# Raw float32 scores for the first 14 head pairs, and theta and channel weights split by column blocks

## The chip, the cores and the metric

The kernel runs on one core of one Trainium2 chip. The metric is device time of one execution in microseconds (us); below, the time of a kernel is the median of its runs. The engines are named as the profile names them: PE (TensorE, matmuls; PEld its weight loads), DVE (VectorE), ACT (ScalarE), POOL (GpSimd) and SP (SyncE, which issues all DMAs here).

## The reference

Attention with soft-capped scores over 8 batches of 12 heads (448 tokens, 64 channels a head), and then a block that mixes tokens and channels:

```python
scores = cap * np.tanh(scale * (q @ k.T) / cap)
attn = softmax(scores)                       # over the last axis
x = concat_heads(attn @ v)                   # (8, 448, 768)

theta = x @ w_theta                          # 768 x 768
zr, zi = x * cos(theta), x * sin(theta)
u = x + w_tok_r @ zr + w_tok_i @ zi          # over the 448 tokens
out = u + max(u @ w_ch, 0)                   # 768 x 768
```

All inputs and the output are float32. `q` and `k` are drawn 5.5 times, `w_theta` and `w_tok_i` 8 times as large as usual.

## The kernel before

**Formats.** A matmul in float32 proper (`F32`) is issued as two instructions; one in `fp32r` (`F32R`) is issued as one, with operands of fewer bits. Where the kernel wants float32 accuracy from fp32r it splits each operand into `hi` (rounded to fp32r) and `lo` (the rest) and adds three products, hi·hi + lo·hi + hi·lo. Scores, theta, token mixing and the channel projection are done so. `attn @ v` (tile `a`, L229) and the sums of the exponentials (tile `r`, L244, a product with a column of ones) are products in float32 proper.

**Weights.** The host passes each weight matrix as words that hold more than float32, and the kernel makes `hi` and `lo` from them on the chip. A `Split` has three steps: `load` (a DMA on SP), `scale` (one pass on ACT, L99) and `split` (six passes on DVE and the rounding to `hi`, which ACT does for the channel weights, L109, and DVE for the others, L111). There are 6 pieces of theta weights (`th0` to `th5`, each 128 rows of the matrix), 7 of token weights (`tk0` to `tk6`) and 6 of channel weights (`c00` to `c02` for the left half of the columns, `c10` to `c12` for the right, each 256 rows). Theta and channel pieces pass through `g_sb[0]` and `g_sb[1]`, which theta also uses for its angles, so that two such pieces at most are in flight; token pieces pass through the buffers of `zh` and `zl`.

**Pairs and steps.** Work on attention goes by pairs of heads, `k` = 0 to 47, six for each batch. The pipeline runs in steps `s`: step `s` computes the scores of pair `s` in two halves (`qk_half`, tile `s`, L190, then tanh from PSUM to SBUF, L191, on ACT), and `attn @ v` and the sums of pair `s - 1`. The two heads of a pair lie on partitions 0 to 63 and 64 to 127, so that each score matmul uses 64 rows of the array. A half has 2 chunks x 3 products x 2 heads = 12 matmuls. Scores have one PSUM tile (4 banks), so that a half can start when the tanh of the half before is done. The exponentials (`exp_half`, L197) follow on ACT, the reciprocal of the sums (L271) every second step on DVE.

The first 8 steps (`FIRST`) do attention alone. From step 8 on, steps come in groups of six, one group for a batch (`part` 0 to 5): theta in parts 0 and 1, transposes and token mixing in parts 1 to 3, the channel projection in parts 4 and 5, each beside the attention of pair `s`. So batch 0 has its theta in steps 8 and 9 and its channel projections in steps 12 and 13.

**q and k.** `load_qk(k)` brings a pair into the one buffer `qk_sb`; `prep(k)` makes `hi[k]` and `lo[k]` from it on DVE (L176, L177) and then issues the load of the next pair. In the start, `prep` runs two steps ahead, later one.

**Order.** The order is written by hand, and each engine and the DMA queue take their instructions in that order. In a step: `qk_half(s, 0)`; weights at "a" (in the start only); `exp_half(s, 0)` (in the start); `av(s - 1)`; the load of v; sums; `qk_half(s, 1)`; `prep`; weights at "b"; the reciprocal; the script of the part, with the exponentials in it; weights at "c" ahead of the script's last item. The table `WEIGHTS` says which steps of which pieces stand there: `>` is load, `*` is scale, a bare name is split.

Of the kernel before, what the change touches and what calls it, by code (L numbers as in the profile page):

```python
# [12 lines left out]
F32 = mybir.dt.float32  # L13
F32R = mybir.dt.float32r
I32 = mybir.dt.int32
U32 = mybir.dt.uint32
AF = mybir.ActivationFunctionType
ALU = mybir.AluOpType

P = 128  # L20
# [6 lines left out]
FIRST = 8  # L27

DIRECT = 10


@with_exitstack
def softcap_attn_then_spectral_mix(ctx, tc, qk2, v, cap, w_theta, w_tok, w_ch, ident, outT):
    nc = tc.nc
    B, NP, P, _, S = qk2.shape
    D = P // 2
    CP = v.shape[2]
    NCH = S // CP
    DM = NP * P
    NJ = DM // P  # L40
    NC2 = 2 * S // P
    NS = B * NP

    const = ctx.enter_context(tc.tile_pool(name="const", bufs=1))
    wk = ctx.enter_context(tc.tile_pool(name="wk", bufs=2))
    psS = ctx.enter_context(tc.tile_pool(name="psS", bufs=1, space=bass.MemoryType.PSUM))
    psM = ctx.enter_context(tc.tile_pool(name="psM", bufs=4, space=bass.MemoryType.PSUM))

    w_theta, w_tok = (w.bitcast(I32).rearrange("j p (n two) -> j p n two", two=2) for w in (w_theta, w_tok))
    w_ch = w_ch.bitcast(I32).rearrange("h j p (n two) -> h j p n two", two=2)  # L50


    cap_sb = const.tile([P, 1], F32, name="cap_sb")
# [11 lines left out]
    wth_h = const.tile([P, NJ, DM], F32R, name="wth_h")  # L65
    wth_l = const.tile([P, NJ, DM], F32R, name="wth_l")
    wch_h = const.tile([P, NJ, DM], F32R, name="wch_h")
    wch_l = const.tile([P, NJ, DM], F32R, name="wch_l")
# [6 lines left out]
    qk_sb = const.tile([P, 2, S], F32, name="qk_sb")  # L75
# [36 lines left out]
            nc.vector.tensor_tensor(t, t, hi.bitcast(F32), op=ALU.subtract)  # L112
            nc.vector.tensor_tensor(lo, t, lw, op=ALU.add)

    def room_g(a, n, i):
        def room():
            st = g_sb[i % 2].rearrange("p x y s -> p (x y s)")
            raw = st[:, : 2 * a * n].rearrange("p (a n two) -> p a n two", a=a, two=2)
            return raw, st[:, 2 * a * n : 3 * a * n].rearrange("p (a n) -> p a n", a=a)
        return room  # L120

    def room_z(n, name):
        def room():
            raw = wk.tile([P, NC2, P], F32, tag="zh", name=f"{name}_raw", bufs=2).rearrange("p c s -> p (c s)")
            t = wk.tile([P, NC2, P], F32, tag="zl", name=f"{name}_t", bufs=2).rearrange("p c s -> p (c s)")
            return raw[:, : 2 * n].rearrange("p (n two) -> p n two", two=2), t[:, :n]
        return room

    hw = DM // 2
    steps = {}  # L130

    def weight_steps():
        for j in range(NJ):
            steps["th", j] = Split(room_g(1, DM, j), w_theta[j].unsqueeze(1), wth_h[:, j : j + 1], wth_l[:, j : j + 1])
        for c in range(NC2):
            steps["tk", c] = Split(room_z(S, f"swk{c}"), w_tok[c], wtk_h[:, c], wtk_l[:, c])
        for half in range(2):
            for i in range(NJ // 2):
                js, cols = slice(2 * i, 2 * i + 2), slice(half * hw, half * hw + hw)
                steps[f"c{half}", i] = Split(room_g(2, hw, half + i), w_ch[half, js].rearrange("a p n two -> p a n two"),  # L140
                                             wch_h[:, js, cols], wch_l[:, js, cols], True)


    WEIGHTS = {
# [6 lines left out]
    }  # L151

    def weights(s, pos):
        for word in WEIGHTS.get((s, pos), "").split():
            step = steps[word[-3:-1], int(word[-1])]
            {">": step.load, "*": step.scale}.get(word[0], step.split)()


    hi, lo, vt, pt, pst, bc = {}, {}, {}, {}, {}, {}
    X = {}  # L160
    state = {}

    def load_qk(k):

        nc.sync.dma_start(qk_sb, qk2[k // NP, k % NP])

    def load_v(k):
        vt[k] = wk.tile([CP, 2, NCH, D], F32, tag="v", name=f"v{k}", bufs=2)
        nc.sync.dma_start(vt[k], v[k // NP, k % NP])

    def prep(k):

        for parts, name in ((hi, "hi"), (lo, "lo")):
            tag, bufs = ("xhl", 6) if k < NP or k == NP + 1 else (name, 1)
            parts[k] = wk.tile([P, 2, S], F32R, tag=tag, name=f"{name}{k}", bufs=bufs)
        nc.vector.tensor_copy(hi[k], qk_sb)  # L176
        nc.vector.tensor_tensor(lo[k], qk_sb, hi[k].bitcast(F32), op=ALU.subtract)  # L177
        if k + 1 < NS:
            load_qk(k + 1)

    def qk_half(k, half):

        sp = psS.tile([P, 2, 2, 512], F32, tag="s", name=f"s{k}_{half}")
        pp = pt[k, half] = wk.tile([CP, 2, 2, S], F32, tag="p", name=f"p{k}_{half}", bufs=3)
        for i in range(2):
            ks = slice((2 * half + i) * CP, (2 * half + i + 1) * CP)
            for n, (kk, qq) in enumerate(((hi, hi), (lo, hi), (hi, lo))):
                for hh in range(2):
                    rows = slice(hh * D, (hh + 1) * D)
                    nc.tensor.matmul(sp[:CP, i, hh, :S], kk[k][rows, 1, ks], qq[k][rows, 0, :], start=n == 0, stop=n == 2)  # L190
        nc.scalar.activation(pp, sp[:CP, :, :, :S], AF.Tanh, scale=qscale[:CP])  # L191

    def exp_half(k, half):
# [30 lines left out]
    def av(k):  # L224
        va = vt.pop(k)
        acc = psM.tile([P, 512], F32, tag="m", name=f"a{k}")
        for c in range(NCH):
            for hh in range(2):
                nc.tensor.matmul(acc[hh * D : (hh + 1) * D, :S], va[:, hh, c, :], pt[k, c // 2][:, c % 2, hh, :],  # L229
                                 start=c == 0, stop=c == NCH - 1)  # L230
        x = wk.tile([P, S], F32, tag="x", name=f"x{k}", bufs=12)
        nc.scalar.copy(x, acc[:, :S])
        X[k // NP, k % NP] = x
# [132 lines left out]
    def us(b, j):  # L366
        split_x(b, j, "us")

    def pipeline(general):
        state["general"] = general  # L370
        load_v(0)
        prep(0)
        for step in (("tk", 0), ("tk", 1)):
            steps[step].load()

        prep(1)
        for s in range(FIRST + 6 * B):
            k = s - 1
            b, part = divmod(s - FIRST, 6)
            live = s < NS  # L380
            start = s < FIRST
            if s + 2 < FIRST:
                prep(s + 2)
            elif s == FIRST - 1:
                prep(FIRST)
            if live:
                qk_half(s, 0)
            if start:
                weights(s, "a")
                exp_half(s, 0)  # L390
            if 0 <= k < NS:
                av(k)
            if not start and part == 4:
                for j in range(NJ // 2, NJ):
                    us(b, j)
            if s + 1 < NS:
                load_v(s + 1)
            if 0 <= k < NS:
                sums(k, (0,) if start else (0, 1))
                if not start:  # L400
                    invert(k)
            if live:
                qk_half(s, 1)
            if 0 <= k and start:
                sums(k, (1,))
            if not start and s + 1 < NS:
                prep(s + 1)
            weights(s, "b")
            if 0 <= k and start:
                invert(k)  # L410
            script = ["B", "a", "b"] if start else part_scripts(b)[part]
            for i, e in enumerate(script):
                if not start and i == len(script) - 1:
                    weights(s, "c")
                    if s % 2 == 1 and s <= NS + 1:
                        norm(s - 3)
                        norm(s - 2)
                if isinstance(e, str):
                    if live:
                        if e in "AB":  # L420
                            exp_half(s, "AB".index(e))
                        else:
                            add_half(s, "ab".index(e))
                else:
                    e[0](b, e[1])
            if start:
                weights(s, "c")
                for n in {4: (0, 1), 5: (2, 3), 7: (4, 5)}.get(s, ()):
                    norm(n)
                for j in {6: range(4), 7: range(4, NJ)}.get(s, ()):  # L430
                    split_x(0, j, "xs")
# [50 lines left out]
```

## Time and profile before

| | |
|---|---|
| median of 3 runs | 1002.59 us (1002.05 to 1004.07) |
| the profiled execution | 1001.84 us, its span 999.8 us |
| mean granted TensorE clock | 0.987 |
| busy: PE, DVE, ACT | 961.5, 654.1, 598.1 us |
| q and k loads (L165) | 48 of 448 KB, 3.4 us to landing |
| theta and channel weight loads (L95) | 12 of 768 KB, 4.2 and 4.6 us to landing |

The profile is that of one execution; its time is set beside its span, which goes from the first to the last instruction on the core. A row of the order of time reads: start, length, engine, line, operation, output <- inputs, partitions x columns and shape, count, and in brackets how long the engine had been idle and what ended it. Neighbouring instructions of one kind are merged into a row, the length then reaching from the first start to the last end. `L190` is line 190 of the kernel before.

### The profile page before, as it was taken

What the parts mean: (1) busy time and instruction counts of PE and PEld (TensorE: products, weight loads), DVE (VectorE), ACT (ScalarE), POOL (GpSimd) and SP (SyncE); (2) the same over time, 40 slices, a digit from 0 to 9 for tenths busy, and PEclk for the clock granted to TensorE, in tenths of its full rate; (3) what the DMA queues carried; (4) which work ended last, traced back from release to release, by engine and by line L of the source; (5) the groups of instructions that cost most, each with busy time, mean ns of one, the idle gap of its engine ahead of it and who ended that gap; (6) DMA issues with size and microseconds to landing.
All of it is one profiled execution on the core that took longest, in us unless ns stands there. A gap on an engine that the chain in (4) does not pass through costs nothing.

```text
span 999.8 us, 12973 instructions
## 1 busy us (share of the span) xinstructions
PE 961.5 (96%) x5304; PEld 709.9 (71%) x5304; DVE 654.1 (65%) x893; ACT 598.1 (60%) x615; POOL 0.4 (0%) x6
## 2 busy tenths in 40 slices
PE   6988998969999999999999999999999999999897
PEld 2433676747677777877877877776778677789897
DVE  4999777777676568656585576675586566753551
ACT  5868586455765468646775567745784567642520
POOL 0000000000000000000000000000000000000000
PEclk9998999979999999999999999999999999999999
DMA  5654112332111321122111321222210230102001
GB/s 194 199 190 133 47 32 93 96 100 74 38 47 37 102 68 54 37 74 82 48 48 37 102 65 37 65 52 81 72 48 29 83 92 28 28 5 71 1 1 59
DMA packets 31508, 68.70 MB, mean 69 GB/s; under 512 B 4304, under 2 KB 16720, under 8 KB 31440
## 3 DMA queue, kind: packets, MB, share of 16 engines
q1 hardware_dynamic: 31440, 67.78, 22.0%
q8 instruction: 44, 0.72, 0.3%
q14 instruction: 24, 0.20, 0.1%
HBM read 45.74 MB, written 11.01 MB: 57 GB/s over the span
## 4 chain that ended last, share of the span: by engine, by line
PE 68%; DVE 17%; ACT 11%; issue 2%; DMA 2%; SPq 0%; DVEq 0%; ACTq 0%
PE a L229 10%; PE s L190 9%; PE mx L337 6%; PE ch L295 6%; PE mx L339 6%; PE mx L338 6%; PE ch L296 6%; PE ch L297 6%; PE th L295 3%; PE th L296 3%; PE th L297 3%; DVE ri L271 3%; ACT p L197 2%; PE t L328 2%; ACT p L191 2%
## 5 line engine op out<-in xcount | busy, mean ns | idle before, releaser
L191 ACT ACTIVATE p<-s,qscale 112x1792 f32<-112x1792 f32 x96 | 168.6, 1757 | 179.4 <-PE s L190 179.4
L197 ACT ACTIVATE p<-p,cap_sb 112x1792 f32<-112x1792 f32 x96 | 170.5, 1789 | 0.5
L229 PE MATMUL a<-p,v 112*64 112x448 f32 x768 | 156.6, 550 | 1.3 <-ACT p L197 1.3
L337 PE MATMUL mx<-wtk_h,zh 128*128 128x448 f32 x336 | 127.7, 380 | 2.8 <-DVE zl L330 2.8
L339 PE MATMUL mx<-wtk_h,zl 128*128 128x448 f32 x336 | 124.0, 369 | 0.0
L338 PE MATMUL mx<-wtk_l,zh 128*128 128x448 f32 x336 | 123.9, 369 | 0.0
L229 PEld LDWEIGHTS a<-p,v 112*64 112x64 f32 x768 | 51.2, 138 | 85.5 <-issue 76.9
L295 PE MATMUL ch<-us,wch_h 128*128 128x448 f32 x288 | 107.5, 373 | 0.0
L295 PE MATMUL th<-xs,wth_h 128*128 128x448 f32 x288 | 107.0, 371 | 0.0
L190 PE MATMUL s<-hi 64*112 64x448 f32 x384 | 81.6, 420 | 25.4 <-ACT p L191 19.5
L296 PE MATMUL ch<-us,wch_h 128*128 128x448 f32 x288 | 105.8, 367 | 0.0
L297 PE MATMUL ch<-us,wch_l 128*128 128x448 f32 x288 | 105.8, 367 | 0.0
L297 PE MATMUL th<-xs,wth_l 128*128 128x448 f32 x288 | 105.3, 366 | 0.0
L296 PE MATMUL th<-xs,wth_h 128*128 128x448 f32 x288 | 105.3, 366 | 0.0
L190 PEld LDWEIGHTS s<-hi 64*112 64x112 f32 x384 | 34.5, 176 | 80.6 <-issue 31.3
L222 DVE TENSOR_TENSOR ps<-ps,p 112x896 f32<-112x896 f32 x76 | 82.6, 1087 | 1.3
L271 DVE RECIPROCAL ri<-r 128x448 f32<-128x448 f32 x24 | 70.8, 2952 | 10.3 <-PE r L244 10.3
L176 DVE CAST hi<-qk_sb 128x896 fp32r<-128x896 f32 x48 | 28.7, 599 | 74.5 <-PE s L190 65.0
L308 DVE SCALAR_TENSOR_TENSOR g_sb<-g_sb 128x448 f32<-128x448 f32 x48 | 30.0, 625 | 70.9 <-ACT g_sb L307 70.6
L190 PE MATMUL s<-hi,lo 64*112 64x448 f32 x384 | 72.9, 375 | 0.4 <-DVE lo L177 0.4
L190 PE MATMUL s<-lo,hi 64*112 64x448 f32 x384 | 72.8, 373 | 0.0
L348 DVE SCALAR_TENSOR_TENSOR x<-ch,x 128x448 f32<-128x448 f32 x48 | 29.8, 621 | 64.5 <-PE ch L297 64.5
(67 smaller groups left out, 1462.5 us busy)
## 6 DMA issues: line engine op xcount, KB each, us to landing
qk_sb<-in_qk SPq DMA_DIRECT2D x48, 448.0 KB, 3.4
v<-in_v SPq DMA_DIRECT2D x48, 224.0 KB, 2.5
bc<-ri SPq DMA_DIRECT2D x96, 112.0 KB, 2.3
out_dram<-x SPq DMA_DIRECT2D x48, 224.0 KB, 1.9
g_sb<-in_wth SPq DMA_DIRECT2D x6, 768.0 KB, 4.2
g_sb<-in_wch SPq DMA_DIRECT2D x6, 768.0 KB, 4.6
swk_raw<-in_wtok SPq DMA_DIRECT2D x7, 448.0 KB, 3.7
ident_sb<-in_ident SPq DMA_DIRECT2D x1, 64.0 KB, 2.5
```

The costliest lines, as they stand in the source:

```text
L190: nc.tensor.matmul(sp[:CP, i, hh, :S], kk[k][rows, 1, ks], qq[k][rows, 0, :], start=n == 0, stop=n == 2)
L191: nc.scalar.activation(pp, sp[:CP, :, :, :S], AF.Tanh, scale=qscale[:CP])
L197: nc.scalar.activation(pp, pp, AF.Exp, scale=cap_sb[:CP])
L222: nc.vector.tensor_tensor(pst[k], pst[k], pt[k, 1][:, i], op=ALU.add)
L229: nc.tensor.matmul(acc[hh * D : (hh + 1) * D, :S], va[:, hh, c, :], pt[k, c // 2][:, c % 2, hh, :], start=c == 0, stop=c == NCH - 1)
L271: nc.vector.reciprocal(ri, r[:, :S])
L295: nc.tensor.matmul(acc[:, :S], wh[:, j, ms], t[:, 0, :], start=j == 0, stop=False)
L296: nc.tensor.matmul(acc[:, :S], wh[:, j, ms], t[:, 1, :], start=False, stop=False)
L297: nc.tensor.matmul(acc[:, :S], wl[:, j, ms], t[:, 0, :], start=False, stop=j == NJ - 1)
L337: nc.tensor.matmul(acc[:, :S], zh[:, c, :], wtk_h[:, c, :], start=c == 0, stop=False)
L338: nc.tensor.matmul(acc[:, :S], zh[:, c, :], wtk_l[:, c, :], start=False, stop=False)
L339: nc.tensor.matmul(acc[:, :S], zl[:, c, :], wtk_h[:, c, :], start=False, stop=c == NC2 - 1)
```

## The change

1. For k < 14 (`WHOLE`) the scores are one product of the raw q and k in float32 proper: 4 products a half instead of 12 fp32r ones. `prep` is left out for these pairs. Pair 0 is loaded to `qk_sb` as before; pairs 1 to 13 go to the two buffers of `hi` and `lo` in turn; the load of pair s + 2 is issued after `qk_half(s, 1)`. From pair 14 on everything is as before.
2. Theta and channel weights are cut into blocks of 128 output columns with all 768 rows (`th0` to `th5`, `ch0` to `ch5`), so that projection `m` needs piece `m` alone. The host lays the words out so that a block is contiguous on each partition. A piece has 768 elements a partition, as before.
3. The table `WEIGHTS` has other slots, among them (7,"a"), (9,"a") and (13,"b"); weights at "a" now exist after the start too, behind `av`.

```diff
+WHOLE = 14
...
-    w_theta, w_tok = (w.bitcast(I32).rearrange("j p (n two) -> j p n two", two=2) for w in (w_theta, w_tok))
-    w_ch = w_ch.bitcast(I32).rearrange("h j p (n two) -> h j p n two", two=2)
+    w_tok = w_tok.bitcast(I32).rearrange("c p (n two) -> c p n two", two=2)
+    w_theta, w_ch = (w.bitcast(I32).rearrange("m p j (n two) -> m p j n two", two=2) for w in (w_theta, w_ch))
...
     def weight_steps():
-        for j in range(NJ):
-            steps["th", j] = Split(room_g(1, DM, j), w_theta[j].unsqueeze(1), wth_h[:, j : j + 1], wth_l[:, j : j + 1])
+        for m in range(NJ):
+            ms = slice(m * P, (m + 1) * P)
+            steps["th", m] = Split(room_g(m), w_theta[m], wth_h[:, :, ms], wth_l[:, :, ms])
+            steps["ch", m] = Split(room_g(m), w_ch[m], wch_h[:, :, ms], wch_l[:, :, ms], True)
...
-        for half in range(2):
-            for i in range(NJ // 2):
-                js, cols = slice(2 * i, 2 * i + 2), slice(half * hw, half * hw + hw)
-                steps[f"c{half}", i] = Split(room_g(2, hw, half + i), w_ch[half, js].rearrange("a p n two -> p a n two"),
-                                             wch_h[:, js, cols], wch_l[:, js, cols], True)
...
         (2, "a"): "*th2", (2, "b"): "th2 >th4", (2, "c"): "*tk1", (3, "a"): "*th3", (3, "b"): "tk1 >tk3 th3 >th5",
-        (4, "a"): "*th4", (4, "b"): "th4 >c00", (4, "c"): "*tk2", (5, "a"): "*th5", (5, "b"): "tk2 >tk4 th5 >c01",
-        (5, "c"): "*tk3 *tk4", (6, "b"): "tk3 >tk5", (6, "c"): "*c00", (7, "b"): "tk4 >tk6", (7, "c"): "*tk5 c00 *c01 *tk6",
-        (8, "b"): "tk5", (8, "c"): "c01", (9, "c"): "tk6", (10, "c"): ">c02", (11, "b"): "*c02 c02 >c11",
-        (11, "c"): ">c10 *c11", (12, "b"): "c11 *c10 c10 >c12", (12, "c"): "*c12 c12",
+        (3, "c"): "*tk2", (4, "a"): "*th4", (4, "b"): "th4 >ch0", (4, "c"): "*tk3", (5, "b"): "tk2 >tk4 tk3 >tk5",
+        (5, "c"): "*th5", (6, "b"): "th5 >ch1", (6, "c"): "*tk4", (7, "a"): "*ch0", (7, "b"): "tk4 >tk6 ch0", (7, "c"): "*tk5",
+        (8, "b"): "tk5", (8, "c"): "*tk6 tk6 *ch1", (9, "a"): "ch1", (10, "c"): ">ch2", (11, "b"): "*ch2 ch2 >ch4",
+        (11, "c"): ">ch3", (12, "b"): "*ch3 ch3 >ch5", (12, "c"): "*ch4 ch4", (13, "b"): "*ch5 ch5",
...
     def load_qk(k):
 
-        nc.sync.dma_start(qk_sb, qk2[k // NP, k % NP])
+        if 0 < k < WHOLE:
+            raw[k] = wk.tile([P, 2, S], F32, tag=("hi", "lo")[k % 2], name=f"qk{k}", bufs=1)
+        else:
+            raw[k] = qk_sb
+        nc.sync.dma_start(raw[k], qk2[k // NP, k % NP])
...
-        for parts, name in ((hi, "hi"), (lo, "lo")):
-            tag, bufs = ("xhl", 6) if k < NP or k == NP + 1 else (name, 1)
-            parts[k] = wk.tile([P, 2, S], F32R, tag=tag, name=f"{name}{k}", bufs=bufs)
-        nc.vector.tensor_copy(hi[k], qk_sb)
-        nc.vector.tensor_tensor(lo[k], qk_sb, hi[k].bitcast(F32), op=ALU.subtract)
+        hi[k] = wk.tile([P, 2, S], F32R, tag="hi", name=f"hi{k}", bufs=1)
+        lo[k] = wk.tile([P, 2, S], F32R, tag="lo", name=f"lo{k}", bufs=1)
+        nc.vector.tensor_copy(hi[k], raw[k])
+        nc.vector.tensor_tensor(lo[k], raw[k], hi[k].bitcast(F32), op=ALU.subtract)
...
-            for n, (kk, qq) in enumerate(((hi, hi), (lo, hi), (hi, lo))):
+            products = ((raw, raw),) if k < WHOLE else ((hi, hi), (lo, hi), (hi, lo))
+            for n, (kk, qq) in enumerate(products):
                 for hh in range(2):
                     rows = slice(hh * D, (hh + 1) * D)
-                    nc.tensor.matmul(sp[:CP, i, hh, :S], kk[k][rows, 1, ks], qq[k][rows, 0, :], start=n == 0, stop=n == 2)
+                    nc.tensor.matmul(sp[:CP, i, hh, :S], kk[k][rows, 1, ks], qq[k][rows, 0, :],
+                                     start=n == 0, stop=n == len(products) - 1)
...
-            if s + 2 < FIRST:
-                prep(s + 2)
-            elif s == FIRST - 1:
-                prep(FIRST)
...
             if 0 <= k < NS:
                 av(k)
+            if not start:
+                weights(s, "a")
...
-            if not start and s + 1 < NS:
+            if s + 2 <= WHOLE:
+                load_qk(s + 2)
+            if WHOLE <= s + 1 < NS:
                 prep(s + 1)
             weights(s, "b")
```

More of the change, by code (lines that the diff above doesn't have):

```diff
@@ L113, in split, with room_g @@
             nc.vector.tensor_tensor(lo, t, lw, op=ALU.add)
-    def room_g(a, n, i):
+    def room_g(i):
         def room():
             st = g_sb[i % 2].rearrange("p x y s -> p (x y s)")
-            raw = st[:, : 2 * a * n].rearrange("p (a n two) -> p a n two", a=a, two=2)
-            return raw, st[:, 2 * a * n : 3 * a * n].rearrange("p (a n) -> p a n", a=a)
+            raw = st[:, : 2 * DM].rearrange("p (j n two) -> p j n two", j=NJ, two=2)
+            return raw, st[:, 2 * DM : 3 * DM].rearrange("p (j n) -> p j n", j=NJ)
         return room
@@ L127, in room_z @@
         return room
-    hw = DM // 2
     steps = {}
     def weight_steps():
-        for j in range(NJ):
-            steps["th", j] = Split(room_g(1, DM, j), w_theta[j].unsqueeze(1), wth_h[:, j : j + 1], wth_l[:, j : j + 1])
+        for m in range(NJ):
+            ms = slice(m * P, (m + 1) * P)
+            steps["th", m] = Split(room_g(m), w_theta[m], wth_h[:, :, ms], wth_l[:, :, ms])
+            steps["ch", m] = Split(room_g(m), w_ch[m], wch_h[:, :, ms], wch_l[:, :, ms], True)
         for c in range(NC2):
             steps["tk", c] = Split(room_z(S, f"swk{c}"), w_tok[c], wtk_h[:, c], wtk_l[:, c])
-        for half in range(2):
-            for i in range(NJ // 2):
-                js, cols = slice(2 * i, 2 * i + 2), slice(half * hw, half * hw + hw)
-                steps[f"c{half}", i] = Split(room_g(2, hw, half + i), w_ch[half, js].rearrange("a p n two -> p a n two"),
-                                             wch_h[:, js, cols], wch_l[:, js, cols], True)
     WEIGHTS = {
@@ L161, in softcap_attn_then_spectral_mix @@
     state = {}
+    raw = {}
     def load_qk(k):
-        nc.sync.dma_start(qk_sb, qk2[k // NP, k % NP])
+        if 0 < k < WHOLE:
[3 more added lines that the diff above has]
+        nc.sync.dma_start(raw[k], qk2[k // NP, k % NP])
     def load_v(k):
@@ L371, in pipeline @@
         load_v(0)
-        prep(0)
+        load_qk(1)
         for step in (("tk", 0), ("tk", 1)):
             steps[step].load()
-        prep(1)
         for s in range(FIRST + 6 * B):
@@ L456, with words, blocks @@
     CP, P = 112, 128
-    DM = H * D
-    def rows(w):
+    def words(w):
         return np.ascontiguousarray(w).view(np.int64).reshape(-1, P, w.shape[1])
+    def blocks(w):
+        return np.ascontiguousarray(words(w).reshape(-1, P, w.shape[1] // P, P).transpose(2, 1, 0, 3))
     q, k = (t.transpose(0, 1, 3, 2).reshape(B, H // 2, 2 * D, S) for t in (q, k))
@@ L467 @@
         "in_cap": np.ascontiguousarray(cap).reshape(1, 1),
-        "in_wth": rows(moe_w_theta),
-        "in_wtok": rows(np.concatenate([moe_w_tok_r.T, moe_w_tok_i.T], axis=0)),
-        "in_wch": np.stack([rows(moe_w_ch[:, : DM // 2]), rows(moe_w_ch[:, DM // 2 :])]),
+        "in_wth": blocks(moe_w_theta),
+        "in_wtok": words(np.concatenate([moe_w_tok_r.T, moe_w_tok_i.T], axis=0)),
+        "in_wch": blocks(moe_w_ch),
     }
```

## The prediction

> **What bounds the kernel now.** I read the profile from the top: the page's busy shares first, then a table of stretches cut at the starts of the steps (a step `s` of the pipeline begins where its first score matmul starts), then TensorE's order of time for the idle times in it.
>
> ```profile
> PE 961.5 (96%) x5304; PEld 709.9 (71%) x5304; DVE 654.1 (65%) x893; ACT 598.1 (60%) x615; POOL 0.4 (0%) x6
> PE   6988998969999999999999999999999999999897
> ```
>
> TensorE (PE) is busy for 96% of the span, and in the 40 slices it falls below 9 only in the first nine, plus twice at the end. So the kernel is bound by TensorE; time can be won only where PE stands still, and any work added to PE costs its full length. The change touches the steps 0 to 13, and the table by steps (columns: stretch, length, busy time of PE, PEld, DVE, ACT, POOL with counts, granted clock, DMA) shows what each has to give:
>
> ```profile
> core 0: us, PE busy (x) PEld busy (x) DVE busy (x) ACT busy (x) POOL busy (x), PEclk, DMA share, GB/s
> 27.68:65.77 38.09, 37.21 (x226) 15.15 (x226) 37.06 (x47) 33.63 (x27) 0.00 (x0) 1.00 0.55 180
> 65.77:82.99 17.22, 11.58 (x56) 4.63 (x57) 16.24 (x28) 9.42 (x8) 0.00 (x0) 0.80 0.55 178
> ...
> 114.40:135.47 21.07, 21.07 (x118) 14.73 (x117) 10.29 (x16) 15.78 (x16) 0.00 (x0) 1.00 0.11 33
> ...
> 160.64:185.48 24.84, 22.19 (x118) 17.50 (x117) 18.64 (x25) 13.04 (x15) 0.00 (x0) 0.93 0.26 92
> 203.56:232.15 28.59, 19.90 (x95) 14.81 (x94) 19.96 (x26) 15.56 (x15) 0.00 (x0) 0.82 0.28 92
> 330.35:347.53 17.18, 17.18 (x96) 13.08 (x96) 7.50 (x10) 9.88 (x10) 0.00 (x0) 1.00 0.23 81
> ```
>
> The rows are steps 2 to 5 together, then step 6, 9, 11, 13 and, for comparison, step 19, which does the same PE work as step 13 one batch later. Steps 2 to 5 take 38.09/4 = 9.52 us each with PE and DVE both full. Step 6 takes 17.22, which is 7.70 more than such a step. Step 13 takes 28.59 against 17.18 in step 19, 11.41 more. Step 9 has no idle PE at all. The idle times themselves:
>
> ```profile
> 77.66 0.71 PE L190 MATMUL s<-hi 64*112 64x448 f32 x2 [5.64 <-ACT p L191]
> ...
> 101.78 0.46 PE L190 MATMUL s<-hi 64*112 64x448 f32 x2 [1.49 <-ACT p L191]
> ...
> 174.97 0.90 PE L328 MATMUL t<-ident_sb,g_sb 128*128 128x128 f32 x3 [2.65 <-DVE zl L330]
> ...
> 206.36 3.40 PE L229 MATMUL a<-p,v 112*64 112x448 f32 x16 [1.33 <-ACT p L197]
> 217.12 0.72 PE L190 MATMUL s<-hi 64*112 64x448 f32 x2 [7.36 <-ACT p L191]
> ```
>
> The bracket is PE's idle time before the row and what ended it. These five, in steps 6, 8, 11, 12/13 and 13, are all that the weights' preparation costs after the start; the rest of an over-long step (7.70 - 5.64 = 2.06 in step 6, 11.41 - 7.36 - 1.33 = 2.72 in step 13) goes with the lower granted clock of that row (0.80, 0.82).
>
> **The change, part by part.**
>
> *One float32 product for three.* For k < 14 a half of the scores is 4 float32 products (2 chunks x 2 heads) instead of 12 fp32r ones. What each costs PE is read from a step without a stall:
>
> ```profile
> 56.26 0.46 PE L190 MATMUL s<-hi 64*112 64x448 f32 x2 [0.22 <-ACT p L191]
> 56.55 0.36 PE L190 MATMUL s<-hi,lo 64*112 64x448 f32 x2
> ...
> 57.65 3.23 PE L229 MATMUL a<-p,v 112*64 112x448 f32 x16
> 60.80 1.70 PE L244 MATMUL r<-p,ones_sb 112*32 112x448 f32 x8
> 62.43 0.46 PE L190 MATMUL s<-hi 64*112 64x448 f32 x2
> ...
> 63.85 1.70 PE L244 MATMUL r<-p,ones_sb 112*32 112x448 f32 x8
> ...
> 65.77 0.46 PE L190 MATMUL s<-hi 64*112 64x448 f32 x2 [0.22 <-ACT p L191]
> ```
>
> A half of the scores now lasts 57.65 - 56.26 = 1.39 and 63.85 - 62.43 = 1.42, so 1.41 us for 12 matmuls. `r<-p` and `a<-p` are true float32: each product is two instructions (8 for the 4 products of an `r` half, 16 for the 8 of `a`), so it is not one matmul for three but two for three. The `r` half streams the same 448 columns, in the same number of float32 products, in two pairs that run side by side: 62.43 - 60.80 = 1.63. `a` agrees: (60.80 - 57.65)/8 = 0.39 a product. That the two heads of a pair run side by side is seen in the weight loads of `a`, which come two at a time, 0.37 apart:
>
> ```profile
> 29.52 0.14 PEld L229 LDWEIGHTS a<-p,v 112*64 112x64 f32 x2 [0.23 <-issue]
> 29.89 0.14 PEld L229 LDWEIGHTS a<-p,v 112*64 112x64 f32 x2 [0.23 <-issue]
> ```
>
> The trace holds no float32 product on 64 rows. In `a` and `r` the pair splits the array's columns, in the scores its rows. fp32r shows that row halves do run side by side (row 56.26 to row 56.55: two started in 0.29, later ones each 0.20). Bounds: nothing more than now, 1.41, if the two passes overlap fully; 4 products one after the other at 0.75 (two passes of 0.375) plus 0.13 to begin, 3.13, if they don't. I take 1.63, the nearest row: same dtype, same count, same columns. That is **+0.22 us a half, slower on PE**; 28 halves, 3 of them in the cold start below, so 25 x 0.22 = **+5.5**.
>
> *No hi/lo split for k < 14.* DVE loses a cast and a subtraction per pair, 1.60 us (195.68 to 197.28 below), and they are off PE's path except where they delay the weights. In step 9 PE never waits, so there it is worth nothing. k = 0 starts without them:
>
> ```profile
> 5.89 0.71 PE L190 MATMUL s<-hi 64*112 64x448 f32 x2 [5.89 <-DVE hi L176]
> 7.01 0.71 PE L190 MATMUL s<-hi,lo 64*112 64x448 f32 x2 [0.41 <-DVE lo L177]
> ...
> 15.50 0.71 PE L190 MATMUL s<-hi 64*112 64x448 f32 x2 [1.85 <-ACT p L191]
> ...
> 18.01 4.77 PE L229 MATMUL a<-p,v 112*64 112x448 f32 x16
> ```
>
> The first scores can start when q and k land, some 0.7 us earlier (the cast is 0.6), and the 0.41 wait goes. But these three halves run cold (18.01 - 15.50 = 2.51 for what takes 1.41 later), and by the warm difference doubled and the fixed part kept, float32 takes some 3.2: +0.7 each, +2.1 together, less 1.1, is +1.0 at `a`. As `a` is itself half cold, about half of that is given back when the clock comes at its own time. I take **+0.4**, bounds -0.5 and +1.5.
>
> *Loads of q and k.* They go to two buffers, two steps ahead, on SP's queue, behind the same loads of v and ahead of the weights'. Each is issued after the second half of step s and due at the start of step s + 2, a whole step of 9.5 us or more later; hidden. The loads of weights are as many and as large as before.
>
> *Step 6.* ACT stood still here, and the tanh behind it, because a scale of token weights waited for a load that had been issued late:
>
> ```profile
> 75.36 0.61 ACT L99 ACTIVATE swk_raw<-swk_raw 128x448 f32<-128x448 f32 x1 [7.30 <-DMA swk_raw<-in_wtok]
> ...
> 83.77 0.91 ACT L99 ACTIVATE g_sb<-g_sb 128x768 f32<-128x768 f32 x1
> 84.58 1.95 ACT L286 CAST xs<-x 128x448 fp32r<-128x448 f32 x4
> 86.43 1.74 ACT L191 ACTIVATE p<-s,qscale 112x1792 f32<-112x1792 f32 x1
> 88.20 1.79 ACT L197 ACTIVATE p<-p,cap_sb 112x1792 f32<-112x1792 f32 x1
> 89.90 0.51 ACT L232 COPY x<-a 128x448 f32<-128x448 f32 x1
> ```
>
> In the old table tk4 is loaded in (5,"b") and scaled in (5,"c"); in the new one it is loaded in (5,"b") and scaled in (6,"c"), a step later, and every other slot before it has at least a step between load and scale. DVE, whose splits release those loads, had 37.06/4 = 9.3 us of work in a step of 9.5 and gets 1.60 less, so it no longer lags. **-7.70**, the clock's part included.
>
> *Step 7.* What is late next: ACT. In step 6 it does tk4's scale (0.6) and four xs casts (1.95) after an exp that ends 11.6 us into the step (the second tanh starts at 8.04 = 1.63 + 3.15 + 1.63 + 1.63; 1.75 and 1.79 follow). With steps of 9.52 + 0.44 the casts end 4.2 into step 7; tanh to 5.9, the new scale of ch0 in (7,"a") to 6.8, exp to 8.6, copy to 9.1, second tanh to 10.9. PE wants that bank at 8.04 + 1.63 = 9.7, and waits 0.22 in any step: **+1.0** (bounds 0 and 2.5).
>
> *Step 8.* The 1.49 came from xs casts, ahead of tanh on ACT, that waited for DVE. Two splits of q and k fewer ahead of them (3.2 us): gone, **-1.5** (bound 0).
>
> *Step 11.* The 2.65 stays. Its cause is the same in both tables, the split of a channel piece in (11,"b") ahead of `zl` on DVE:
>
> ```profile
> 169.31 0.56 DVE L104 TENSOR_SCALAR g_sb<-g_sb 128x768 int32<-128x768 int32 x1 [0.82 <-ACT g_sb L99]
> ...
> 174.23 1.15 DVE L330 TENSOR_TENSOR zl<-t,zh 128x512 fp32r<-128x512 f32 x2
> ```
>
> DVE was idle before it and waited for ACT's scale, which stands behind the second tanh; the split's 4.9 us then delay `zl`. Removing the q/k split here only lengthens DVE's idle time. **0** (bound -4.4).
>
> *Steps 12 and 13.* Before, (12,"b") splits two channel pieces, loads a third, and (12,"c") scales it at once:
>
> ```profile
> 195.68 0.56 DVE L176 CAST hi<-qk_sb 128x896 fp32r<-128x896 f32 x1
> ...
> 197.28 0.56 DVE L104 TENSOR_SCALAR g_sb<-g_sb 128x768 int32<-128x768 int32 x1
> ...
> 202.20 0.55 DVE L104 TENSOR_SCALAR g_sb<-g_sb 128x768 int32<-128x768 int32 x1
> ```
> ```profile
> 212.09 0.88 ACT L99 ACTIVATE g_sb<-g_sb 128x768 f32<-128x768 f32 x1 [4.10 <-DMA g_sb<-in_wch]
> ```
>
> A split is 202.20 - 197.28 = 4.92 of DVE; the load is issued behind two of them, ACT waits 4.10 for it, and PE 7.36 for the tanh behind. The new table scales ch4 (loaded in 11) there, and ch5 a step later. On the old clock, with ch3's split where the q/k split stood: DVE 195.7 to 200.6; its cast on ACT, after two of DVE's passes (1.5) and at 0.9 for a pass of that size, to 198.1; two exps to 201.7, ch4's scale to 202.6. DVE first has three additions of p (1.09 each) and two shorter ones of results:
>
> ```profile
> L222 DVE TENSOR_TENSOR ps<-ps,p 112x896 f32<-112x896 f32 x76 | 82.6, 1087 | 1.3
> ```
>
> So it begins ch4 at about 205 (200.6 + 3.3 and about one), and the cast that ACT waits for ends at 205 + 1.5 + 0.9 = 207.4. The tanh behind ends at 209.1, where PE, after scores (1.63) and `a` (3.15) from 204.0, wants it at 208.8. Instead of 11.41 a stall of about 0.3 is left: **-11.1**. ch5 is scaled after the second tanh (209.1 + 1.63 + 1.75 = 212.5), so its split ends at 212.5 + 0.9 + 4.9 = 218.3. A projection takes (17.18 - 2 x 1.41 - 3.15)/3 = 3.7 in step 19, so the third of step 13 begins at 210.7 + 7.4 = 218.1 and needs the low part two matmuls (0.4) later. There is the least slack; a miss costs what it misses, up to 5.
>
> *Column blocks.* The block of a projection needs all rows of its own columns, so the last block is due latest; blocks, not halves, let ch5 be split in step 13 at all. Each split handles the same 768 elements a partition, in runs of 128: priced as before.
>
> The sum: 5.5 + 0.4 - 7.7 + 1.0 - 1.5 + 0 - 11.1 = **-13.4**. The profiled execution took 1001.84 us (span 999.8), 0.75 under the median of 1002.59. 1001.84 - 13.4 = 988.4; as a median, 989.
>
> **The rivals.**
>
> *Row halves don't run side by side in float32 (slower).* Then a half is 3.13 in place of 1.63, 1.50 more on PE in each of 28: 989 + 42 = **1031**. It decides against the change from a half of 1.63 + 13.4/28 = 2.1 us on. For it: no row of the trace has this form. Against: fp32r in row halves, and float32 in column halves, both do it.
>
> *The two passes of a product keep their order.* If the second head's first pass must wait until the first head's second pass has begun, a half is one pass longer, 1.63 + 0.375 = 2.0, and 28 x 0.375 = 10.5 is lost: **999.5**. Against: `a` and `r` have the same order of calls, and their loads come in twos. The Trainium skill, page "TensorE: Matmul & The Clock Gate", section "Part 3: Packing small matmuls", says that matmuls start and end strictly in program order. By that rule this rival would hold if the passes stand product by product in the program; the paired loads (0.37 apart, two at once) say that for columns they don't, and no row here shows it for rows.
>
> *The weights' stalls come back elsewhere.* The new slots put cast and tanh in one queue as before: if ch5 is late by its whole landing and step 7 and 13 wait as step 8 did, some 9 are lost: **998**. For it: ACT's chain in step 7 has no slack. Against: between load and scale there is now a step everywhere.
>
> *Float32 on row halves costs PE no more than now.* 25 x 0.22 less: **983**.
>
> **How the numbers follow.** My forecast has 0.70 (its own range, by the bounds of the start, of step 7 and of step 13's slack, 985 to 994); the ordered passes 0.09, the returned stalls 0.08, serial row halves 0.10, the cheap product 0.03. What can be told from no change here is 0.2%, 2 us. Faster: 0.70 + 0.03 and nearly all of 0.17 = 0.86; the same 0.04; slower 0.10. The range of 8 in 10 goes from 983 to 1000, which leaves out the serial case and the tails.
>
> **What would show it.** In the changed kernel a half of the scores in step 4 or 5 is 8 matmuls in 1.63, PE's starts two at a time 0.375 apart; steps 2 to 5 are 9.96 long; step 6 loses its 5.64 and its low clock; before step 8 there is a wait of about 1.2 on tanh; step 11 keeps 2.65; step 13 is about 18 long with a wait of at most 1 on a tanh. From step 14 on nothing moves. I am wrong if a half is 2 us or more, or if a wait on `g_sb` loads or on ch5's split stands in step 13.

## The result, and the profile after

The changed kernel takes 984.45 us (984.10 to 986.33, 4 runs) against 1002.32 us before (4 runs): a ratio of 0.9824, 95% interval 0.9805 to 0.9844. The forecast was 989, with a range of 983 to 1000. The profiled execution took 984.10 us, 17.74 less than the one before; the prediction's sum for the same pair was -13.4.

The page after, the rows that answer to those of before:

```profile
PE 960.3 (98%) x5192; PEld 695.0 (71%) x5192; DVE 631.7 (64%) x865; ACT 597.1 (61%) x615; POOL 0.4 (0%) x6
PE   6999998999999999999999999999999999999897
PEclk9999999999999999999999999999999999999999
```

PE's busy time hardly moved (961.5 to 960.3), and two things cancel in it: the scores of 14 pairs take longer, and fewer matmuls run at a lowered clock (mean granted clock 0.987 before, 0.997 now). The rest of the shorter span is idle time: 38.3 us of the span before (999.8 - 961.5), 22.0 now (982.3 - 960.3). By stretches (columns as in the prediction; steps 2 to 5, 6, 7, 9, 10, 11, 13 of the changed kernel):

```profile
core 0: us, PE busy (x) PEld busy (x) DVE busy (x) ACT busy (x) POOL busy (x), PEclk, DMA share, GB/s
...
25.67:66.04 40.37, 39.46 (x193) 12.32 (x193) 34.36 (x47) 33.28 (x27) 0.00 (x0) 1.00 0.60 190
66.04:76.13 10.09, 9.86 (x48) 3.08 (x49) 8.03 (x13) 8.21 (x7) 0.00 (x0) 1.00 0.48 155
76.13:86.52 10.39, 9.86 (x48) 3.08 (x48) 10.15 (x15) 10.39 (x12) 0.00 (x0) 1.00 0.66 213
...
107.40:129.04 21.64, 21.64 (x110) 14.06 (x109) 12.07 (x21) 15.99 (x16) 0.00 (x0) 1.00 0.10 32
129.04:154.00 24.96, 24.96 (x134) 17.08 (x133) 16.64 (x23) 17.87 (x20) 0.00 (x0) 1.00 0.24 78
154.00:178.12 24.12, 21.48 (x110) 15.52 (x109) 16.92 (x23) 12.14 (x14) 0.00 (x0) 1.00 0.28 95
...
196.76:214.75 17.99, 17.89 (x87) 12.31 (x86) 16.28 (x21) 11.87 (x12) 0.00 (x0) 1.00 0.32 112
```

A step of the start is now 10.09 long (40.37/4) instead of 9.52, and so is step 6, which took 17.22. Step 13 takes 17.99 instead of 28.59. Step 9 is 0.57 longer. These two kinds of numbers, longer plain steps and two long steps that became plain, are the change. TensorE's order of time shows the price and the waits that are left:

```profile
5.21 3.33 PE L194 MATMUL s<-qk_sb 64*112 64x448 f32 x8 [5.21 <-DMA qk_sb<-in_qk]
...
15.58 1.76 PE L194 MATMUL s<-qk 64*112 64x448 f32 x8 [1.86 <-ACT p L196]
17.27 3.23 PE L234 MATMUL a<-p,v 112*64 112x448 f32 x16
...
62.42 1.76 PE L194 MATMUL s<-qk 64*112 64x448 f32 x8
64.11 1.70 PE L249 MATMUL r<-p,ones_sb 112*32 112x448 f32 x8
...
86.52 1.76 PE L194 MATMUL s<-qk 64*112 64x448 f32 x8 [0.53 <-ACT p L196]
...
168.89 0.55 PE L333 MATMUL t<-ident_sb,g_sb 128*128 128x128 f32 x3 [2.64 <-DVE zl L335]
```

A half of the scores is 8 instructions and lasts 64.11 - 62.42 = 1.69, 0.28 more than the 1.41 of 12 fp32r matmuls. Of the five waits of before only step 11's is left; at the start of step 8 PE waits 0.53, where a plain step waits 0.23.

### The profile page after: what moved, and what is told of

Read it like the earlier page. It is cut to its first block, busy times and chain, and to the rows that moved or that the text cites. A ratio compares the mean times of both kernels' runs of the same rounds, so it can differ in the third digit from the quotient of the medians.

```text
span 982.3 us, 12716 instructions
## 1 busy us (share of the span) xinstructions
PE 960.3 (98%) x5192; PEld 695.0 (71%) x5192; DVE 631.7 (64%) x865; ACT 597.1 (61%) x615; POOL 0.4 (0%) x6
## 4 chain that ended last, share of the span: by engine, by line
PE 78%; ACT 11%; DVE 9%; issue 2%; DMA 0%; SPq 0%; DVEq 0%
PE a L234 13%; PE s L194 13%; PE mx L342 6%; PE mx L343 6%; PE mx L344 6%; PE ch L300 6%; PE ch L302 6%; PE ch L301 6%; PE th L300 4%; PE th L301 4%; PE th L302 4%; ACT p L196 3%; PE r L249 3%; PE t L333 3%; ACT p L202 2%; DVE ri L276 2%
## 5 line engine op out<-in xcount | busy, mean ns | idle before, releaser
L342 PEld LDWEIGHTS mx<-wtk_h,zh 128*128 128x128 f32 x336 | 63.6, 189 | 9.6 <-DVE zl L335 4.2
L344 PEld LDWEIGHTS mx<-wtk_h,zl 128*128 128x128 f32 x336 | 63.5, 189 | 5.3
L343 PEld LDWEIGHTS mx<-wtk_l,zh 128*128 128x128 f32 x336 | 63.6, 189 | 4.8
L335 DVE TENSOR_TENSOR zl<-t,zh 128x512 fp32r<-128x512 f32 x96 | 55.0, 615 | 18.1 <-ACT zh L334 18.1
L345 DVE TENSOR_TENSOR x<-mx,x 128x448 f32<-128x448 f32 x48 | 29.8, 622 | 55.2 <-PE mx L344 54.6
```

What stands on the lines that cost most here:

```text
L342: nc.tensor.matmul(acc[:, :S], zh[:, c, :], wtk_h[:, c, :], start=c == 0, stop=False)
L343: nc.tensor.matmul(acc[:, :S], zh[:, c, :], wtk_l[:, c, :], start=False, stop=False)
L344: nc.tensor.matmul(acc[:, :S], zl[:, c, :], wtk_h[:, c, :], start=False, stop=c == NC2 - 1)
```

## The experiments

Theory: float32 scores cost PE about 0.57 us a pair and pay by what they take off DVE; the slots pay by step 13. Rivals: all of the gain is the slots'; or all of it is DVE's relief.

**The slots alone.** The new weights' pieces and table, with the scores as before:

```diff
-            products = ((raw, raw),) if k < WHOLE else ((hi, hi), (lo, hi), (hi, lo))
+            products = ((hi, hi), (lo, hi), (hi, lo))   # for all k, with prep and load_qk as before the change
```

> The new weights' blocks and slots, with the scores as before (three fp32r products, q and k split on DVE). Mine: DVE has its 1.60 us a pair back, so the first eight steps stay bound by DVE and end where they ended before the change (step 8 starts at 91 to 92.5); the long wait of step 13 is gone but for about 2 us, as the split of q and k stands ahead of ch3's on DVE again: 992 us. Rival (all of the gain is the slots', and float32 only costs PE, 0.57 us a pair as measured): 984.4 - 14 x 0.57 = 976.5 us.

994.58 us, ratio 0.9920 (0.9901 to 0.9940). Step 6 is a plain step here too. But DVE does not get through, and the waits come in steps 7 and 8 instead. PE's order of time, and the table for steps 7, 8 and 10:

```profile
88.96 0.71 PE L188 MATMUL s<-hi 64*112 64x448 f32 x2 [4.84 <-DVE hi L174]
...
97.69 2.14 PE L227 MATMUL a<-p,v 112*64 112x448 f32 x8 [2.31 <-ACT p L195]
```
```profile
74.83:88.96 14.13, 9.29 (x57) 3.82 (x58) 13.85 (x20) 10.37 (x11) 0.00 (x0) 0.99 0.47 147
88.96:116.74 27.78, 25.15 (x110) 15.00 (x111) 23.14 (x36) 14.93 (x16) 0.00 (x0) 0.82 0.32 89
137.82:162.23 24.41, 24.41 (x141) 17.77 (x141) 18.12 (x25) 17.86 (x20) 0.00 (x0) 1.00 0.26 80
```

PE waits for `hi` of pair 8 itself, on a DVE that is busy for 13.85 of 14.13 us, and the clock falls (0.82). So the slots alone don't repair the start: the rival's 976.5 is refuted. My 992 was 2.6 too low, by the waits in steps 7 and 8; step 13 kept about the wait of 2 that I had given it (2.33, the step 19.64 long). Step 10 is 24.41 with fp32r scores, against 25.17 before: that 0.76 is the slots', as tk6's split no longer stands in (9,"c"), where DVE ran it ahead of step 10's first `zl`. The pieces and the slots were not tried apart.

**The float32 scores alone**, with the old pieces and slots:

```diff
+            products = ((raw, raw),) if k < WHOLE else ((hi, hi), (lo, hi), (hi, lo))   # WEIGHTS, room_g, weight_steps as before
```

> The raw float32 scores for k < 14, with the weights' pieces and slots of before. Mine: step 6 loses its wait of 5.64 through DVE's relief alone (tk4's load is issued in time though it is scaled in the same step), step 13 keeps most of its wait (two splits ahead of the load of the piece that is scaled at once), about 9.5 us more than with the new slots: 993.5 us. Rival 1 (the new slots removed the wait of step 6): that one stays too, 1001 us. Rival 2 (float32 only costs): 1002.3 + 8 = 1010 us.

992.87 us, ratio 0.9910 (0.9884 to 0.9935), as forecast to 0.6. Step 6 is 10.09 long with the old slots too: ACT now waits 0.40 for tk4, where it had waited 7.30. Step 13 keeps its wait:

```profile
69.14 0.64 ACT L101 ACTIVATE swk_raw<-swk_raw 128x448 f32<-128x448 f32 x1 [0.40 <-DMA swk_raw<-in_wtok]
...
203.76 0.88 ACT L101 ACTIVATE g_sb<-g_sb 128x768 f32<-128x768 f32 x1 [4.01 <-DMA g_sb<-in_wch]
```
```profile
208.79 3.33 PE L198 MATMUL s<-qk 64*112 64x448 f32 x8 [6.62 <-ACT p L200]
```

So either half of the change removes step 6's wait; only float32 scores keep DVE from falling behind in steps 7 and 8; only the slots remove step 13's. The two halves bring 8.2 and 10.0 us, and together 17.9.

**Float32 for all pairs.**

```diff
-WHOLE = 14
+WHOLE = 48
```

> Raw float32 scores for all 48 pairs. Mine: from step 14 on PE has no idle time to win and DVE's relief is worth nothing, so each of the 34 further pairs costs the measured 2 x 0.28 us: 984.4 + 19 = 1003.5 us. Rival (the longer scores cost little where ACT's tanh, not PE, ends the wait for the next half): below 990 us.

997.93 us, ratio 0.9959 (0.9943 to 0.9976): 13.5 more than the changed kernel, not 19, and far from the rival's 990. Each later step is 0.56 longer, as forecast, but for the third of each batch, which is 0.33 shorter (23.64 to 23.31). PE shows no idle time there, because `r`'s row hides it. The step's `r` in the changed kernel, then with float32 for all:

```profile
255.34 1.83 PE L249 MATMUL r<-ps,ones_sb 112*32 112x448 f32 x8
```
```profile
255.87 1.56 PE L249 MATMUL r<-ps,ones_sb 112*32 112x448 f32 x8
```

Eight such instructions take 0.96 in most steps and 1.83 here: the last four start only when DVE's sums are done, and the busy time counts the gap. DVE after that, in the changed kernel, and with float32 for all:

```profile
262.09 0.56 DVE L179 CAST hi<-qk_sb 128x896 fp32r<-128x896 f32 x1
262.68 1.09 DVE L180 TENSOR_TENSOR lo<-qk_sb,hi 128x896 fp32r<-128x896 f32 x1
263.69 1.15 DVE L335 TENSOR_TENSOR zl<-t,zh 128x512 fp32r<-128x512 f32 x2
```
```profile
262.35 1.09 DVE L335 TENSOR_TENSOR zl<-t,zh 128x512 fp32r<-128x512 f32 x2
```

Without the q/k split ahead of it `zl` starts 1.34 earlier on the clock of each kernel, and mixing needs it. That these two rows make up the 0.89 of the step is argued from them, not tried by itself. My "DVE's relief is worth nothing" was wrong for one step in six.

**Float32 for k < 9.**

```diff
-WHOLE = 14
+WHOLE = 9
```

> Raw float32 scores for k < 9 instead of k < 14. Mine: five pairs give back 0.57 us each on PE (-2.9), but their splits of q and k are on DVE again in steps 8 to 12: about +0.8 in step 10 and +1.8 in steps 12 and 13, where casts ahead of tanh wait for DVE: 984 us. Rival (DVE's relief is worth nothing after the start): 981.5 us.

985.71 us, ratio 0.9839 (0.9819 to 0.9859): not told apart from the changed kernel. Steps 9, 10 and 12 are 0.56 shorter, so the +0.8 that I gave step 10 didn't come. Step 13 is 1.62 longer, by a wait that wasn't there, which speaks against the rival; in step 11 the clock fell after the same idle time:

```profile
202.97 0.46 PE L194 MATMUL s<-hi 64*112 64x448 f32 x2 [2.32 <-ACT p L196]
```
```profile
152.91:177.91 25.00, 22.36 (x118) 17.52 (x117) 18.61 (x25) 12.15 (x14) 0.00 (x0) 0.93 0.26 90
```

**Float32 for k < 9 and k = 13.**

```diff
-WHOLE = 14
+RAW = {*range(9), 13}
```

> Raw float32 scores for k = 0 to 8 and 13 only; 9 to 12 split as before. Mine: the splits in steps 8 to 11 lie beside idle DVE and cost nothing, those four pairs give back 0.57 us each on PE, and pair 13 keeps DVE free ahead of ch3 in step 12, so that step 13 stays at 18: 982.2 us (1.4 more if the clock falls in step 11 as it did with raw scores for k < 9). Rival (it is the number of splits taken from DVE that counts, not the one in step 12): 985.5 us, as with k < 9.

982.66 us, ratio 0.9815 (0.9797 to 0.9833). Steps 11 and 13:

```profile
152.06:177.01 24.95, 22.30 (x119) 17.59 (x118) 18.64 (x25) 12.15 (x14) 0.00 (x0) 0.93 0.27 91
195.09:213.31 18.22, 17.86 (x87) 12.31 (x86) 16.50 (x22) 11.74 (x12) 0.00 (x0) 1.00 0.34 124
```

Step 13 loses nearly all of its wait (18.22 against 19.62), so of the later splits only that of pair 13, which stands on DVE ahead of ch3 in step 12, had a cost. Against the changed kernel the 1.8 us lie within the intervals; its step 11 fell to the lower clock.

**ch4 loaded late.**

```diff
-(11, "b"): "*ch2 ch2 >ch4",  (12, "b"): "*ch3 ch3 >ch5",
+(11, "b"): "*ch2 ch2",       (12, "b"): "*ch3 ch3 >ch4 >ch5",
```

> The changed kernel with one load moved: ch4 is loaded in (12,b), behind ch3's split, instead of in (11,b), and still scaled in (12,c). Mine (it is the load right ahead of its scale that cost step 13 its wait): the load is issued at 193.6 and lands 4.9 later, so the scale ends at 199.4 instead of 195.1; by way of the split's first two passes and the cast, tanh ends near 203.6, where PE wants it at 201.7: a wait of about 2 in step 13, 986.4 us. Rival (the two splits side by side on DVE were the cause, not the load's slot): no change, 984.5 us.

984.65 us, ratio 0.9820 (0.9805 to 0.9836): no difference, against my 986.4. ACT in this kernel, and then in the changed one:

```profile
201.34 0.92 ACT L101 ACTIVATE g_sb<-g_sb 128x768 f32<-128x768 f32 x1 [3.00 <-DMA g_sb<-in_wch]
203.87 0.83 ACT L111 CAST wch_h<-g_sb 128x768 fp32r<-128x768 f32 x1 [1.62 <-DVE g_sb L107]
```
```profile
199.23 0.83 ACT L111 CAST wch_h<-g_sb 128x768 fp32r<-128x768 f32 x1 [4.09 <-DVE g_sb L107]
```

The scale does wait 3.00 for the load. But in the changed kernel the cast behind it waits 4.09 for DVE anyway, and of the late landing only 0.65 is left in step 13 (18.64 against 17.99). My theory of the late load was at best a small part.

**Two splits in a step, and three.** First ch3 and ch4 side by side in (12,"b"), then ch5 in the same step as well:

```diff
-(12, "b"): "*ch3 ch3 >ch5", (12, "c"): "*ch4 ch4", (13, "b"): "*ch5 ch5",
+(12, "b"): "*ch3 ch3 *ch4 ch4 >ch5",               (13, "b"): "*ch5 ch5",   # two_splits
+(12, "b"): "*ch3 ch3 *ch4 ch4 >ch5", (12, "c"): "*ch5 ch5",                 # scale_at_once
```

> The changed kernel with ch3 and ch4 split one behind the other in (12,b), as the kernel before did with c11 and c10, and ch5 loaded behind both; ch5 is still scaled a step later, in (13,b). Mine, after the load of ch4 alone was worth only 0.65: what cost step 13 its wait was a scale on ACT, ahead of tanh, of a piece whose load had to wait for both splits; with the scale a step later the two splits are harmless: 984.5 us, no wait over 1 in step 13. Rival (two splits side by side on DVE make the exponentials and tanh late by themselves): a wait of 5 or more in step 13, 990 us.

985.06 us, ratio 0.9823 (0.9803 to 0.9843); step 13 is 17.77 long, with no wait. Two splits are harmless.

> two_splits with one thing more: ch5 is scaled and split in (12,c), the step in which its load is issued, as the kernel before did with c12. Mine: this alone brings the wait of step 13 back: 6 to 7 us of idle PE ahead of the second scores, step 13 about 26 long as with the old slots, 992.5 us. Rival (in the changed kernel DVE is free enough that the scale lands in time): under 987 us.

990.51 us, ratio 0.9893 (0.9875 to 0.9911); step 13 is 25.21 long. SP, ACT and PE:

```profile
192.41 0.33 SPq L97 DMA_DIRECT2D g_sb<-in_wch  x1
```
```profile
197.99 0.92 ACT L101 ACTIVATE g_sb<-g_sb 128x768 f32<-128x768 f32 x1
202.99 0.83 ACT L111 CAST wch_h<-g_sb 128x768 fp32r<-128x768 f32 x1 [4.07 <-DVE g_sb L107]
203.73 1.75 ACT L196 ACTIVATE p<-s,qscale 112x1792 f32<-112x1792 f32 x1
```
```profile
205.53 3.33 PE L194 MATMUL s<-qk 64*112 64x448 f32 x8 [5.00 <-ACT p L196]
```

The wait is back, but not by the load: ch5 needs ch3's buffer only, its load went out at 192.41, and the scale at 197.99 waited for nothing. What ACT waits for is the third split of that step, which stands on DVE behind the sums of p and whose cast stands on ACT ahead of tanh. So the cause of step 13's wait is the third piece in step 12. The load, which in the old table had to wait for the second split, most likely made it longer (6.62 with it in the float32-only kernel, whose pieces also differ, 5.00 here).

**ch2 split later.** To the remaining wait of step 11:

```diff
-(11, "b"): "*ch2 ch2 >ch4", (11, "c"): ">ch3",
+(11, "c"): ">ch3 *ch2 ch2 >ch4",
```

> The changed kernel with ch2's scale and split moved from (11,b) to (11,c), behind the transposes' zl on DVE. Mine: the wait of 2.64 in step 11 goes and nothing else waits, since ch2 is due in step 12's last projection: 981.8 us. Rival (the wait moves: the casts on ACT or zl of the second transposes come late instead): 984 us or more.

981.05 us, ratio 0.9785 (0.9772 to 0.9799). Step 11 takes 21.08 instead of 24.12. DVE:

```profile
165.19 1.16 DVE L334 TENSOR_TENSOR zl<-t,zh 128x512 fp32r<-128x512 f32 x2 [6.74 <-ACT zh L333]
...
175.22 0.55 DVE L106 TENSOR_SCALAR g_sb<-g_sb 128x768 int32<-128x768 int32 x1
```

`zl` goes as soon as ACT has `zh`, and the split fills DVE ten microseconds later. Nothing else waits.

**Pair 0 split again.**

```diff
-            products = ((raw, raw),) if k < WHOLE else ((hi, hi), (lo, hi), (hi, lo))
+            products = ((raw, raw),) if 0 < k < WHOLE else ((hi, hi), (lo, hi), (hi, lo))
```

> The changed kernel with pair 0 alone split into hi and lo again (three fp32r products). Mine (the start gained 2 us, not the 0.4 lost that I forecast, because float32's longer matmuls fill the cold start and the full clock comes some 5 us earlier): step 1 starts with slow matmuls again and step 2 at about 27.3 instead of 25.7, 986 us. Rival (the start gains only by the two waits for DVE that fall away, 0.7 and 0.4): step 2 at about 26.7 minus what three cheaper halves give back, 984.5 us or less.

986.20 us, ratio 0.9842 (0.9827 to 0.9858), the forecast number; step 2 starts at 27.47. Its rows, and those of the kernel with ch4 loaded late, whose start is the changed kernel's own:

```profile
15.58 3.33 PE L195 MATMUL s<-qk 64*112 64x448 f32 x8 [1.85 <-ACT p L197]
18.84 3.46 PE L235 MATMUL a<-p,v 112*64 112x448 f32 x16
```
```profile
15.50 3.33 PE L194 MATMUL s<-qk 64*112 64x448 f32 x8 [1.85 <-ACT p L196]
18.76 4.44 PE L234 MATMUL a<-p,v 112*64 112x448 f32 x16
```

With an fp32r first pair the scores of step 1 run slow (3.33) where the changed kernel has them at full rate (1.76). But the second fence shows the same slow scores in a kernel that begins with float32. In the ten profiles of kernels that begin with float32, the changed one among them, step 2 starts between 24.5 and 28.4, in five of them from 25.6 to 26.2; in the three that begin with fp32r, at 27.2 to 27.7. That float32 brings the clock earlier is likely from this and not settled, and the time itself (0.9827 to 0.9858) is not told apart from the changed kernel's.

**Both findings together**: ch2 later, and float32 for k < 9 and k = 13.

> Both findings together: ch2 split in (11,c), and raw float32 scores for k = 0 to 8 and 13 only. Mine: ch2_later's 981.05 less four pairs at 0.57 us: 978.8 us; step 11 is 21.1 - 0.56 = 20.5 long. Rival (with q and k split again in step 11, ch2's split at (11,c) comes late and step 12's projection or its reciprocal waits): 981 us or more.

978.30 us, ratio 0.9759 (0.9743 to 0.9774), better than both kernels; the interval lies wholly under that of the changed kernel. Step 11:

```profile
152.83:173.32 20.49, 20.49 (x118) 16.23 (x117) 13.95 (x19) 11.33 (x13) 0.00 (x0) 1.00 0.21 72
```

Steps 9 to 12 are each some 0.56 shorter than with ch2 later alone, as forecast. But step 13 is 18.64 long instead of 18.07, by a wait of 0.78 on tanh that neither forecast nor rival had, so that the steps bring 1.7 of the 2.3; that the sum came out is in part luck.

## Why the prediction was right, by its steps

The sign and the mechanism held: PE's own work grew, and two long steps became plain. The terms, forecast and then measured as the step's change less the 0.57 that every step pays:

| step of the sum | forecast | measured |
|---|---|---|
| float32, 25 warm halves | +5.5 (0.22 each) | +7.0 (0.28 each) |
| start | +0.4 | -2.3 |
| step 6 | -7.7 | -7.7 |
| step 7 | +1.0 | +0.3 |
| step 8 | -1.5 | -1.6 |
| step 10 | 0 | -0.8 |
| step 11 | 0 | -1.3 |
| step 13 | -11.1 | -11.2 |
| sum | -13.4 | -17.6 |

The start is step 2's start, 27.68 to 25.67, less one warm half. Steps 9 (+0.57) and 12 (+0.56), in no row, changed by the price of a pair alone. The time of 984.45 lies inside the range of 983 to 1000, but just outside the 985 to 994 that the forecast gave itself, and nearer to the rival of the cheap product (983) than to 989. That rival is refuted all the same: a half costs 0.28 more, not nothing. Terms that missed both ways made up the total, and two of them, the start and step 11, hang on when the clock rose or fell in one execution, which is luck.

- *The price of a half* was taken from the sums' `r` half, 1.63; it is 1.69. The starts come two at a time, 0.37 to 0.47 apart (62.42 and 62.43, 62.89 and 62.90, 63.27 twice, 63.64 and 63.65): row halves of the array run side by side in float32 here as column halves do, so the serial rival (3.13) and the one of the ordered passes (2.0) fall. The Trainium skill, page "TensorE: Matmul & The Clock Gate", section "Part 3", has matmuls start strictly in program order; the trace agrees only if the two passes of a pair stand crosswise in the program, which it doesn't show.
- *Step 6* was right in size. The later slot and DVE's relief were named together; either alone does it (9.52 long with the slots, 10.09 with float32 scores).
- *Step 13* was right in size, down to the stall of about 0.3 that was left (17.99 is 0.25 over 17.17 + 0.57). Its reason was half wrong: the load right ahead of its scale, put back alone, cost 0.65, the third split in step 12 brought a wait of 5.00 back. ch5's split in step 13, named as the place of least slack, cost nothing that a row shows.
- *The start* was mis-sized by 2.7. I let the clock come at its own time of before; in this profile it was there at 15.58, when step 1 begins, while before it came within `a`, after 18.01. The scatter is as wide as the miss: with step 2 at 28.4, as in the kernel with ch4 loaded late, the start would have measured +0.4, with 24.5 it would have been -3.4.
- *Step 11* kept its 2.64 as forecast, but the clock did not fall after it this time. *Step 10* I held for unchanged, as no row shows idle time in it; the slots took a split out of DVE's way there, a wait of 0.8 that PE's busy time had mostly hidden (25.08 of 25.17 us busy before).

## What to carry to other kernels

Where one engine is full, ask of a change what it does to the others' queues: here more work on PE paid because it took work off DVE in the first steps, where DVE was as full as PE, and at one later pair (13) whose split stood ahead of a weight's. For most other pairs it cost its price. When weights are prepared beside the main work, count how many pieces one step can take, and keep their casts out of the queue ahead of what the main engine waits for. A plain step elsewhere in the same trace with the same work is a good price for what a stall, clock included, is worth: here it gave -7.7 and -11.1, and -7.7 and -11.2 were measured.

## What the runs showed of the hardware

- The granted clock after the same idle time is not the same: after 2.64 to 2.65 us in step 11 it was 1.00 in the changed kernel and 0.93 before and with float32 for k < 9, worth 1.3 us. Of the 11 kernels that keep this wait, 5 show the lower clock in their profile. Near the end, where PE waits 2.83 for `zl`, 11 of all 13 show it; in the kernel with both findings the clock stays at 1.00 there, and its last stretch is 1.5 us shorter. The Trainium skill, page "TensorE: Matmul & The Clock Gate", section "Part 1: The HAM clock gate", has a window that runs freely and so a phase that changes from run to run; the trace agrees. It sets the gap that matters at some 3.4 us; here 2.65 was enough.
- PE's busy time can hide waits: 8 instructions at 1.83 that take 0.96 elsewhere, with no idle time in the table.
- A float32 product costs more PE time here than three in fp32r: 1.69 for 4 products (8 instructions) against 1.41 for 12 matmuls, 448 columns each.
